# A decode block on one core: the last gate loaded with its siblings, and w2 summed in rows of half a block

## The chip, the cores and the metric

The kernel runs on one core of a Trainium2 chip. The metric is the device time of one execution in microseconds; before the change the median of three runs is 242.71 us (242.71 to 242.87).

## The reference

One decode step of a transformer block for 4 sequences with a model width of 512. A condition vector `c` gives six modulation vectors, the last of which, `gb`, is the gate of the second half:

```python
mod = (_silu(c) @ w_mod).reshape(c.shape[0], 6, 1, -1)
sa, ca, ga, sb, cb, gb = (mod[:, 0], mod[:, 1], mod[:, 2], mod[:, 3], mod[:, 4], mod[:, 5])
h = _layernorm(x, axis=-1) * (1 + ca) + sa
x = x + ga * _A_ref(h, A_k_cache, A_v_cache, A_wq, A_wo)
h = _layernorm(x, axis=-1) * (1 + cb) + sb
x = x + gb * _B_ref(h, B_w1, B_w3, B_w2)
```

`_A_ref` is attention of one new token over the last 2048 positions of a cache, with 32 query heads in 8 groups. `_B_ref` is the feed-forward part, `(silu(h @ w1) * (h @ w3)) @ w2` with a hidden width of 1792. All is fp32.

## The kernel before, in words

The kernel reads 101 MB of weights and cache once and computes little on them. It is written engine by engine: each engine has its own instruction list, and they wait for each other with semaphores. TensorE (PE) multiplies, VectorE (DVE) and ScalarE (ACT) do the rest, SyncE (SP) issues nearly all loads into one queue, which serves them in the order of issue.

**Attention.** The 8 groups go through two large buffers, `KV[0]` and `KV[1]`, in pairs, in a loop on PE (`pair`, L332) and ACT. A buffer is loaded again when the group in it has been used: SP waits for `x_done` (L112, L114, L122, L125). When group 6 is done, SP loads the weights of the second half into `KV[0]` (L123, L124); when group 7 is done, into `KV[1]` (L126 to L129).

**Loads of the second half, in this order.** `wm_in` is three parts of `w_mod` (`ga`, `sb`, `cb`; 3072 KB, semaphore `dm`). `f1_in` is w1 and a piece of w3 (4096 KB, `df1`). `f2_in` is the rest of w3 (3072 KB, `df2`). `gw_in` is the last gate's part of `w_mod` and the first four chunks of w2 (2048 KB, `dw[0]`). The rest of w2 follows in pieces. A chunk of w2 is 128 of its 1792 rows, laid out as 512 columns on 128 partitions (256 KB); `W2_CUTS` counts in half chunks of 256 columns, and the pieces after `gw_in` end at 16, 20, 24, 27 and 28: 1024, 512, 512, 384 and 128 KB.

**The second half on the engines, from L391.** PE multiplies the attention output out (bM), then the three parts of the modulation into bank `bX` (L396 to L400): four steps of k, and in each one matmul for every part, which writes its own group of 32 output rows. ACT copies the three parts (L402), DVE makes `x1`, and DVE and ACT the layer norm (`stats`, `rroot`), which ends in `h`; one step of it is ACT's Square on L156. PE spreads `x1` over 128 rows (below), transposes `h` and, when `h2T` is copied (L424), multiplies by f1 into bank `bQ` (L432) and by f2 into `bA` (L442). Between these, ACT copies `g_sb` (L438) and PE turns it. DVE builds the hidden vector `hidT`; its last step is L467, after PE's transposes of `u_sb`.

**w2 and the end.** A result of 4 rows of 512 uses few of the 128 partitions, so the kernel ends in another form: 8 blocks of 64 columns on 128 rows. `spread` (L263) brings a tensor into that form with 8 short matmuls of 64 columns: for each of the four groups of 32 output rows two, one for each half of a block of 128 columns, with the small constant `same` shifted by `half` as weights. The first 8 chunks of w2 (HEAD) are multiplied in long matmuls of 512 columns into bank `bO` (L486), copied to `y_sb` (L496) and spread into `bX` (L502). The gate `gb_sb` comes from four long matmuls into `bM` (L472), is copied by ACT (L475), spread into `bT` (L498) and copied again (`gbJ`, L500). The remaining chunks go straight into `bX` in rows of half a block: 8 matmuls of 64 columns for each chunk, with `half` of `hidT` as weights (L492); the last chunk is split into two halves, each of 4 such matmuls. PE waits for the semaphore of each piece (`dw`, L479). DVE multiplies by `gbJ`, adds `x1J` (L505, L507), and SP stores the output (L509).

Of the kernel before, what the change touches and what calls it, by code (L numbers as in the profile page):

```python
# [10 lines left out]
B, D, HQ, G, SK, DH, W, FF = 4, 512, 32, 8, 8192, 128, 2048, 1792  # L11
P = 128
# [1 line left out]
NT = 4  # L14
EPS = 1e-5
CHUNKS = [(j, c) for c in range(4) for j in range(4) if c < 2 or j < 3]
HEAD = 8

W2_CUTS = [0, 8, 16, 20, 24, 27, 28]
H = 64  # L20
PAIRS = G // 2
W2_AT = 8192
OUT_SHAPE = (P, H)


# [19 lines left out]
        return (self.sem, self.n)  # L45


def block_kernel(nc, x_in, t0_in, t1_in, kv_in, w_in, wm_in, f1_in, f2_in, gw_in, w2_in, out):
    T, v, s, gp, S = nc.tensor, nc.vector, nc.scalar, nc.gpsimd, nc.sync

    def sems(names):
# [2 lines left out]
    def sb(name, cols, rows=P):  # L54
        return nc.alloc_sbuf_tensor(name, (rows, cols), F32).ap()
# [18 lines left out]
    ident, same, eps = sb("ident", P), sb("same", 48), sb("eps", 1)  # L74
    sc, e1, e2 = sb("sc", 16), sb("e1", 16), sb("e2", 16)
    hT, h2T = sb("hT", 16), sb("h2T", 16)
    Z = sb("Z", B * 28)
    q_sb, p_sb, o_sb, a_sb, y_sb, g_sb, u_sb, gb_sb = [sb(n, 512) for n in "q_sb p_sb o_sb a_sb y_sb g_sb u_sb gb_sb".split()]
    pT = sb("pT", NT * B * 16)
    oT = sb("oT", R * B)  # L80
    MX, MT, NM, NB, SM, ST, LS, LR, LB = [sb(n, 32) for n in "MX MT NM NB SM ST LS LR LB".split()]
    sa_sb, ga_sb, sb_sb, cb_sb = [sb(n, 512, B) for n in "sa_sb ga_sb sb_sb cb_sb".split()]
    xc, sq, xs, h, ag, x1 = [sb(n, 512, B) for n in "xc sq xs h ag x1".split()]
    st1, st2 = sb("st1", 8, B), sb("st2", 8, B)
    eT, dT, rT, sT = [sb(n, 64) for n in "eT dT rT sT".split()]
    hidT = sb("hidT", 16 * 48)
    x1J, gbJ, yt, y = [sb(n, H) for n in "x1J gbJ yt y".split()]
    zero = y_sb

    bS, bQ, bT, bP, bO, bX, bA, bM = [bank(n) for n in "bS bQ bT bP bO bX bA bM".split()]  # L90

# [1 line left out]
    def load(dst, src, sem):  # L93
        S.dma_start(dst, src).then_inc(sem, 16)  # L94
# [25 lines left out]
    load(KV[1][:, 8192:14336], kv_in[G - 1][:, 8192:14336], dva)  # L120
    load(KV[1][:, 14336:], kv_in[G - 1][:, 14336:], dvb)
    S.wait_ge(x_done, G - 1)  # L122
    load(KV[0][:, :6144], wm_in, dm)  # L123
    load(KV[0][:, 6144:14336], f1_in, df1)  # L124
    S.wait_ge(x_done, G)  # L125
    load(KV[1][:, :6144], f2_in, df2)  # L126
    load(KV[1][:, 6144:10240], gw_in, dw[0])
    for a, b, sem in zip(W2_CUTS[1:-1], W2_CUTS[2:], dw[1:]):
        load(KV[1][:, W2_AT + a * 256 : W2_AT + b * 256], w2_in[:, (a - 8) * 256 : (b - 8) * 256], sem)  # L129


    l_eps = L.op(gp.memset(eps, EPS))
# [123 lines left out]
    def mm(o, lhsT, rhs, start=True, stop=True):  # L256
        return T.matmul(o, lhsT, rhs, start=start, stop=stop, skip_group_check=True)  # L257
# [144 lines left out]
    t_ga, t_sb, t_cb = [A.op(s.copy(dst, bX[32 * i : 32 * i + B, :])) for i, dst in enumerate((ga_sb, sb_sb, cb_sb))]  # L402
# [12 lines left out]
    spread(bS, same[:B], x1)  # L415
    A.wait((pe, 5))
    t_x1J = A.op(s.copy(x1J, bS[:, :H]))

    T.wait_ge(V.sem, t_h2[1])
    for k in range(4):  # L420
        ins = T.transpose(bT[:, k * B : (k + 1) * B], h[:, k * P : (k + 1) * P], ident[:B, :B])
    ins.then_inc(pe, 1)
    V.wait((pe, 6))
    t_h2T = V.op(v.tensor_copy(h2T, bT[:, :16]))  # L424

    def view(t_):
# [4 lines left out]
    T.wait_ge(df1, 16)  # L431
    for k in range(4):  # L432
        for j in range(4):
            at = 6144 + k * 2048 + j * 512
            ins = mm(bQ[32 * j : 32 * j + B, :], h2T[:, k * B : (k + 1) * B], KV[0][:, at : at + 512], k == 0, k == 3)
    ins.then_inc(pe, 1)
    A.wait((pe, 7))
    t_g = A.op(s.copy(g_sb, bQ))  # L438
    T.wait_ge(A.sem, t_g[1])
    turn(bP, g_sb, pe)  # L440
# [1 line left out]
    for k in range(4):  # L442
        for j in range(3):
            at = k * 1536 + j * 512
            ins = mm(bA[32 * j : 32 * j + B, :], h2T[:, k * B : (k + 1) * B], KV[1][:, at : at + 512], k == 0, k == 3)
    ins.then_inc(pe, 1)
    A.wait((pe, 8))
    t = A.op(s.activation(view(eT), view(bP)[:, :, :, :B], AF.Exp, scale=-1.0))
    V.wait(t)
    t = V.op(v.tensor_scalar(dT, eT, 1.0, None, op0=ALU.add))  # L450
# [6 lines left out]
    hv = hw[:, :, :, 16 : 16 + B]  # L457
    V.wait(l_z)
    V.op(v.tensor_mul(hv[:, 0:2, 3], view(sT)[:, 0:2, 3], view(bP)[:, 2:4, 3, :B]))
    V.wait((pe, 9))  # L460
    t_u = V.op(v.tensor_copy(u_sb[:96], bA[:96]))
    T.wait_ge(V.sem, t_u[1])
    for c in range(4):
        ins = T.transpose(bS[:, c * P : c * P + 96], u_sb[:96, c * P : (c + 1) * P], ident[:96, :96])
    ins.then_inc(pe, 1)
    V.wait((pe, 10))
    t_hid = V.op(v.tensor_mul(hv[:, :, :3], view(sT)[:, :, :3], view(bS)[:, :, :3, :B]))  # L467


    T.wait_ge(dw[0], 16)  # L470
    for k in range(4):
        ins = mm(bM[32 * k : 32 * k + B, :], sc[:, k * B : (k + 1) * B], KV[1][:, 6144 + 512 * k : 6144 + 512 * (k + 1)])  # L472
    ins.then_inc(pe, 1)
    A.wait((pe, 11))
    t_gb = A.op(s.copy(gb_sb, bM))  # L475
    T.wait_ge(V.sem, t_hid[1])
    for i in range(len(W2_CUTS) - 1):
        if i:
            T.wait_ge(dw[i], 16)  # L479
        for n in range(W2_CUTS[i], W2_CUTS[i + 1]):  # L480
            if n < 26 and n % 2:
                continue
            jj, c = CHUNKS[n // 2]
            if n < 2 * HEAD:
                at, k = W2_AT + n * 256, n // 2
                ins = mm(bO[32 * (k % 4) : 32 * (k % 4) + B, :], hv[:, c, jj, :], KV[1][:, at : at + 512], k < 4, k >= HEAD - 4)  # L486
                continue
            for j in range(4):
                for r in (n % 2,) if n >= 26 else (0, 1):
                    at = W2_AT + (n * 256 + j * H if n >= 26 else n * 256 + j * P + r * H)  # L490
                    w = half(hw[:, c, jj, :], r)
                    ins = mm(bX[32 * j : 32 * j + 32, :H], w, KV[1][:, at : at + H], False, n == 27)  # L492
        if i == 1:
            ins.then_inc(pe, 1)
            V.wait((pe, 12))
            t_y = V.op(v.tensor_copy(y_sb, bO))  # L496
            T.wait_ge(A.sem, t_gb[1])
            spread(bT, same, gb_sb)  # L498
            A.wait((pe, 13))
            t_gb = A.op(s.copy(gbJ, bT[:, :H]))  # L500
            T.wait_ge(V.sem, t_y[1])
            spread(bX, same, y_sb, True, False)  # L502
    ins.then_inc(pe, 1)
    V.wait((pe, 14), t_gb)
    t = V.op(v.tensor_mul(yt, bX[:, :H], gbJ))  # L505
    V.wait(t, t_x1J)
    V.op(v.tensor_add(y, yt, x1J), last)  # L507
# [6 lines left out]
def _layout(i):  # L514
    import numpy as np

    def a(t):
        return np.ascontiguousarray(t)

    k = i["A_k_cache"][:, :, SK - W :, :].reshape(B, G, NT, 512, DH)  # L520
    v = i["A_v_cache"][:, :, SK - W :, :].reshape(B, G, NT, 4, P, DH)
    k = k.transpose(1, 4, 2, 0, 3).reshape(G, P, 8192)
    v = v.transpose(1, 4, 2, 0, 3, 5).reshape(G, P, 8192)
    wm = i["w_mod"].reshape(4, P, 6, 512).transpose(1, 0, 2, 3)
    c = i["c"].reshape(B, 4, P).transpose(2, 1, 0).reshape(P, 16)
# [9 lines left out]
    return {  # L535
        "x_in": a(i["A_x"].reshape(B, D)),
        "t0_in": np.concatenate([c, wm[:, :, 1::-1].reshape(P, 4096)], 1),
        "t1_in": np.concatenate([wq[0], wq[1]], 1),
        "kv_in": np.concatenate([k, v], 2),
        "w_in": np.stack([np.concatenate(p, 1) for p in pairs]),  # L540
        "wm_in": a(wm[:, :, 2:5]).reshape(P, 6144),
        "f1_in": np.concatenate([w1, w3[:, :, 1536:]], 2).reshape(P, 8192),
        "f2_in": a(w3[:, :, :1536]).reshape(P, 6144),
        "gw_in": np.concatenate([a(wm[:, :, 5]).reshape(P, 2048), w2[:, : 4 * D]], 1),
        "w2_in": a(w2[:, 4 * D :]),
    }


# [20 lines left out]
```

## Time and profile before

| | us |
|---|---|
| median of three runs | 242.71 |
| the profiled execution | 242.85 |
| its span, first to last instruction | 241.5 |
| PE busy | 135.7 |
| DVE busy | 38.5 |
| ACT busy | 24.2 |

The profile is of one execution; its times are microseconds from the start of the span. A row of a timeline has the start, the duration, the engine, the line, the operation, the tile written and the tiles read, the shapes and the number of instructions merged into the row; in brackets stands the idle time before it and who ended it. An fp32 matmul shows as two passes, so counts in the profile are twice those in the code (transposes are one pass). A row of an issue list has the number of issues, their size and the median time from issue to landing. A row of a list of stages has the stretch, the busy time of each engine, the granted clock of PE as a share of full speed, the busy share of the DMA engines and GB/s.

### The profile page before, as it was taken

How to read it: one execution, taken by the hardware profiler on the slowest of the kernel's cores; microseconds unless marked ns; L12 is line 12 of the kernel's file. 1: busy time of each engine (PE TensorE's matmuls, PEld its weight loads, DVE VectorE, ACT ScalarE, POOL GpSimd, SP SyncE). 2: the span in 40 equal slices, each digit the busy share in tenths (PEclk: the TensorE clock that was granted, in tenths of full speed). 3: DMA queues.
4: the chain of work that ended last, by engine and by line, in shares of the span. 5: the costliest groups of instructions: out<-in, count | busy, mean ns of one | idle time of the engine just before them, and what ended most of it. 6: DMA issues, size and time to landing. Idle time of an engine off the chain costs nothing. (4 is left out here: it accounts for less than half of the span.)

```text
span 241.5 us, 2424 instructions
## 1 busy us (share of the span) xinstructions
PE 135.7 (56%) x1020; PEld 39.1 (16%) x1020; DVE 38.5 (16%) x126; ACT 24.2 (10%) x51; POOL 2.3 (1%) x15
## 2 busy tenths in 40 slices
PE   3004547818773378176613871757228767674885
PEld 0000121301221012012100120112001222111213
DVE  3003202201200022012000220220002222115121
ACT  2002101100110021001200021011000201122100
POOL 3000000000000000000000000000000000000000
PEclk9999958976589599679965699779957997995899
DMA  7998989899989898999898989998989999999992
GB/s 272 446 501 358 510 361 499 369 423 429 516 358 510 358 510 360 429 434 505 369 499 369 499 369 423 434 510 369 499 347 440 436 406 444 452 431 396 431 400 105
DMA packets 3756, 101.30 MB, mean 419 GB/s; under 512 B 548, under 2 KB 676, under 8 KB 1064
## 3 DMA queue, kind: packets, MB, share of 16 engines
q1 hardware_dynamic: 3600, 99.13, 95.6%
q10 hardware_dynamic: 152, 2.11, 2.1%
q8 instruction: 3, 0.05, 0.1%
q14 instruction: 1, 0.01, 0.0%
HBM read 101.20 MB, written 0.03 MB: 419 GB/s over the span
## 5 line engine op out<-in xcount | busy, mean ns | idle before, releaser
L257 PE MATMUL bS<-KV,Z 128*16 128x512 f32 x256 | 42.7, 827 | 41.1 <-PEq L273 41.1
L257 PE MATMUL bO<-KV,pT 128*16 128x512 f32 x256 | 32.9, 658 | 0.5
L257 PEld LDWEIGHTS bS<-KV,Z 128*16 128x16 f32 x256 | 9.2, 123 | 69.1 <-issue 69.1
L220 DVE TENSOR_REDUCE MX<-bS 128x1 f32<-128x512 f32 x8 | 5.5, 692 | 82.2 <-PE bS L257 82.2
L382 ACT ACTIVATE p_sb<-bS,NB 128x512 f32<-128x512 f32 x8 | 5.5, 687 | 103.7 <-ACTq L373 103.7
L291 PE MATMUL bP<-ident,p_sb 128*128 128x128 f32 x32 | 5.5, 298 | 17.3 <-PEq L273 17.3
L257 PE MATMUL bM<-KV,sc 128*4 128x512 f32 x24 | 5.9, 711 | 16.0 <-DVE sc L190 16.0
L257 PE MATMUL bA<-WP,oT 128*4 128x512 f32 x64 | 10.4, 731 | 4.0 <-PEq L273 4.0
L257 PEld LDWEIGHTS bO<-KV,pT 128*16 128x16 f32 x256 | 8.4, 106 | 23.5 <-issue 23.5
L387 ACT ACTIVATE o_sb<-bO,LB 128x512 f32<-128x512 f32 x8 | 5.5, 687 | 48.9 <-ACTq L373 48.9
L291 PE MATMUL bX<-ident,o_sb 128*128 128x128 f32 x32 | 5.0, 280 | 7.8 <-PEq L273 7.8
L246 DVE TENSOR_REDUCE oT<-bX 128x16 f32<-128x64 f32 x8 | 1.8, 224 | 43.7 <-PE bX L291 43.7
L257 PE MATMUL bQ<-WP,hT 128*4 128x512 f32 x64 | 8.3, 592 | 0.6 <-DVE hT L199 0.6
L291 PEld LDWEIGHTS bP<-ident,p_sb 128*128 128x128 f32 x32 | 3.6, 150 | 24.4 <-issue 24.4
L291 PE MATMUL bT<-ident,q_sb 128*128 128x128 f32 x32 | 5.4, 296 | 3.6 <-PEq L273 3.6
L291 PEld LDWEIGHTS bX<-ident,o_sb 128*128 128x128 f32 x32 | 3.4, 140 | 15.0 <-issue 15.0
L229 DVE COPY pT<-bP 128x256 f32<-128x256 f32 x8 | 3.4, 425 | 14.1 <-PE bP L291 14.1
L257 PE MATMUL bQ<-KV,h2T 128*4 128x512 f32 x32 | 5.4, 842 | 0.3 <-DVE h2T L424 0.3
L291 PEld LDWEIGHTS bT<-ident,q_sb 128*128 128x128 f32 x32 | 3.6, 147 | 7.5 <-issue 7.2
L257 PE MATMUL bX<-KV,sc 128*4 128x512 f32 x24 | 4.4, 592 | 0.0
L257 PEld LDWEIGHTS bM<-KV,sc 128*4 128x4 f32 x24 | 0.9, 96 | 20.9 <-DVE sc L190 17.6
L204 DVE TENSOR_REDUCE Z<-bT 128x16 f32<-128x64 f32 x8 | 1.8, 225 | 14.5 <-PE bT L291 14.2
(104 smaller groups left out, 69.2 us busy)
## 6 DMA issues: line engine op xcount, KB each, us to landing
WP<-w_in SPq DMA_DIRECT2D x3, 4096.0 KB, 19.7
KV<-kv_in SPq DMA_DIRECT2D x1, 4096.0 KB, 24.0
KV<-f_in SPq DMA_DIRECT2D x1, 4096.0 KB, 25.6
KV<-kv_in SPq DMA_DIRECT2D x1, 3072.0 KB, 30.8
KV<-wm_in SPq DMA_DIRECT2D x1, 3072.0 KB, 16.3
KV<-f_in SPq DMA_DIRECT2D x1, 3072.0 KB, 18.8
KV<-t_in SPq DMA_DIRECT2D x1, 2056.0 KB, 12.3
WP<-t_in ACTq DMA_DIRECT2D x1, 2048.0 KB, 12.5
```

Of the source, the lines that this page charges most:

```text
L204: v.tensor_reduce(Z.rearrange("p (b i) -> p b i", b=B)[:, :, 12 : 12 + R], bT.rearrange("p (r k i) -> p i r k", r=R, k=4)[:, :B], axis=AX. ...
L220: t = V.op(v.reduce_max(MX[:, 0:1], bS, axis=AX.X))
L229: v.tensor_copy(pT.rearrange("p (t b c r) -> p c b t r", t=NT, b=B, c=4), bP.rearrange("p (c b i) -> p c b i", c=4, b=B)[:, :, :, :16].rea ...
L246: V.op(v.tensor_reduce(oT.rearrange("p (r b) -> p r b", r=R), diag, axis=AX.X, op=ALU.add), ot_ok)
L257: return T.matmul(o, lhsT, rhs, start=start, stop=stop, skip_group_check=True)
L291: ins = T.transpose(dst[:, c * P : (c + 1) * P], src[:, c * P : (c + 1) * P], ident)
L382: A.op(s.activation(p_sb, bS, AF.Exp, bias=NB[:, 0:1], accum_out=SM[:, 0:1]), p_ok)
L387: A.op(s.mul(o_sb, bO, LB[:, 0:1]), o_ok)
```

## The change

The last gate's part of `w_mod` is loaded with the other three in `wm_in`, which has 4096 KB now and fills `KV[0]` together with f1. Its four matmuls go into `bX` beside those of the other parts, as the fourth group of output rows; ACT copies it after the other three, PE spreads it right after `x1`, and ACT copies it into `gbJ` after `x1J`. The tail loses its four matmuls and its spread. w2 begins right behind f2 in `KV[1]`, and its pieces are 16, 8, 3 and 1 half chunks: 2048, 1024, 384 and 128 KB, one load fewer in all. The long matmuls into `bO`, the copy `y_sb` and its spread are gone: all 14 chunks go into `bX` in rows of half a block, 112 matmuls of 64 columns where there were 48. The tile that clears bank `bA` at the start (`zero`) is one of its own.

```diff
-HEAD = 8
-
-W2_CUTS = [0, 8, 16, 20, 24, 27, 28]
+W2_CUTS = [0, 16, 24, 27, 28]
-W2_AT = 8192
+W2_AT = 6144
...
-    load(KV[0][:, :6144], wm_in, dm)
-    load(KV[0][:, 6144:14336], f1_in, df1)
+    load(KV[0][:, :8192], wm_in, dm)
+    load(KV[0][:, 8192:], f1_in, df1)
     S.wait_ge(x_done, G)
     load(KV[1][:, :6144], f2_in, df2)
-    load(KV[1][:, 6144:10240], gw_in, dw[0])
-    for a, b, sem in zip(W2_CUTS[1:-1], W2_CUTS[2:], dw[1:]):
-        load(KV[1][:, W2_AT + a * 256 : W2_AT + b * 256], w2_in[:, (a - 8) * 256 : (b - 8) * 256], sem)
+    for a, b, sem in zip(W2_CUTS[:-1], W2_CUTS[1:], dw):
+        load(KV[1][:, W2_AT + a * 256 : W2_AT + b * 256], w2_in[:, a * 256 : b * 256], sem)
...
     T.wait_ge(dm, 16)
     for k in range(4):
-        for i in range(3):
-            at = (3 * k + i) * 512
+        for i in range(4):
+            at = (4 * k + i) * 512
             ins = mm(bX[32 * i : 32 * i + B, :], sc[:, k * B : (k + 1) * B], KV[0][:, at : at + 512], k == 0, k == 3)
...
-    t_ga, t_sb, t_cb = [A.op(s.copy(dst, bX[32 * i : 32 * i + B, :])) for i, dst in enumerate((ga_sb, sb_sb, cb_sb))]
+    t_ga, t_sb, t_cb, t_gb = [A.op(s.copy(dst, bX[32 * i : 32 * i + B, :])) for i, dst in enumerate((ga_sb, sb_sb, cb_sb, gb_sb))]
...
     t_x1J = A.op(s.copy(x1J, bS[:, :H]))
+    T.wait_ge(A.sem, t_gb[1])
+    spread(bO, same[:B], gb_sb)
+    A.wait((pe, 6))
+    t_gbJ = A.op(s.copy(gbJ, bO[:, :H]))
...
-    T.wait_ge(dw[0], 16)
-    for k in range(4):
-        ins = mm(bM[32 * k : 32 * k + B, :], sc[:, k * B : (k + 1) * B], KV[1][:, 6144 + 512 * k : 6144 + 512 * (k + 1)])
-    ins.then_inc(pe, 1)
-    A.wait((pe, 11))
-    t_gb = A.op(s.copy(gb_sb, bM))
     T.wait_ge(V.sem, t_hid[1])
     for i in range(len(W2_CUTS) - 1):
-        if i:
-            T.wait_ge(dw[i], 16)
+        T.wait_ge(dw[i], 16)
         for n in range(W2_CUTS[i], W2_CUTS[i + 1]):
             if n < 26 and n % 2:
                 continue
             jj, c = CHUNKS[n // 2]
-            if n < 2 * HEAD:
-                at, k = W2_AT + n * 256, n // 2
-                ins = mm(bO[32 * (k % 4) : 32 * (k % 4) + B, :], hv[:, c, jj, :], KV[1][:, at : at + 512], k < 4, k >= HEAD - 4)
-                continue
             for j in range(4):
                 for r in (n % 2,) if n >= 26 else (0, 1):
                     at = W2_AT + (n * 256 + j * H if n >= 26 else n * 256 + j * P + r * H)
                     w = half(hw[:, c, jj, :], r)
-                    ins = mm(bX[32 * j : 32 * j + 32, :H], w, KV[1][:, at : at + H], False, n == 27)
-        if i == 1:
-            ins.then_inc(pe, 1)
-            V.wait((pe, 12))
-            t_y = V.op(v.tensor_copy(y_sb, bO))
-            T.wait_ge(A.sem, t_gb[1])
-            spread(bT, same, gb_sb)
-            A.wait((pe, 13))
-            t_gb = A.op(s.copy(gbJ, bT[:, :H]))
-            T.wait_ge(V.sem, t_y[1])
-            spread(bX, same, y_sb, True, False)
-    ins.then_inc(pe, 1)
-    V.wait((pe, 14), t_gb)
+                    ins = mm(bX[32 * j : 32 * j + 32, :H], w, KV[1][:, at : at + H], n == 0 and r == 0, n == 27)
+    ins.then_inc(pe, 1)
+    V.wait((pe, 12), t_gbJ)
```

How the changed program stands on the queues, word for word, is shown where it is used in the prediction; for SP the stretch of loads changes like this. Before, from the three parts of `w_mod` on:

```order
12 L94 DMA KV<-wm_in 128x6144
13 L94 DMA KV<-f_in 128x8192
14 L94 DMA KV<-f_in 128x6144
15 L94 DMA KV<-gw_in 128x4096
16 L94 DMA KV<-w_in 128x2048
17 L94 DMA KV<-w_in 128x1024 x2
18 L94 DMA KV<-w_in 128x768
19 L94 DMA KV<-w_in 128x256
```

And after, on SP in the same place (w_in is w2, f_in are f1 and f2):

```order
12 L92 DMA KV<-wm_in 128x8192
13 L92 DMA KV<-f_in 128x8192
14 L92 DMA KV<-f_in 128x6144
15 L92 DMA KV<-w_in 128x4096
16 L92 DMA KV<-w_in 128x2048
17 L92 DMA KV<-w_in 128x768
18 L92 DMA KV<-w_in 128x256
```

The gate's 2048 columns have moved from the fourth load into the first, and the two loads of 1024 columns have become part of one of 2048.

More of the change, by code (lines that the diff above doesn't have):

```diff
@@ L45, in op, with block_kernel @@
         return (self.sem, self.n)
-def block_kernel(nc, x_in, t0_in, t1_in, kv_in, w_in, wm_in, f1_in, f2_in, gw_in, w2_in, out):
+def block_kernel(nc, x_in, t0_in, t1_in, kv_in, w_in, wm_in, f1_in, f2_in, w2_in, out):
     T, v, s, gp, S = nc.tensor, nc.vector, nc.scalar, nc.gpsimd, nc.sync
@@ L77, in block_kernel @@
     Z = sb("Z", B * 28)
-    q_sb, p_sb, o_sb, a_sb, y_sb, g_sb, u_sb, gb_sb = [sb(n, 512) for n in "q_sb p_sb o_sb a_sb y_sb g_sb u_sb gb_sb".split()]
+    q_sb, p_sb, o_sb, a_sb, zero, g_sb, u_sb = [sb(n, 512) for n in "q_sb p_sb o_sb a_sb zero g_sb u_sb".split()]
     pT = sb("pT", NT * B * 16)
@@ L81, in block_kernel @@
     MX, MT, NM, NB, SM, ST, LS, LR, LB = [sb(n, 32) for n in "MX MT NM NB SM ST LS LR LB".split()]
-    sa_sb, ga_sb, sb_sb, cb_sb = [sb(n, 512, B) for n in "sa_sb ga_sb sb_sb cb_sb".split()]
+    sa_sb, ga_sb, sb_sb, cb_sb, gb_sb = [sb(n, 512, B) for n in "sa_sb ga_sb sb_sb cb_sb gb_sb".split()]
     xc, sq, xs, h, ag, x1 = [sb(n, 512, B) for n in "xc sq xs h ag x1".split()]
@@ L87, in block_kernel @@
     x1J, gbJ, yt, y = [sb(n, H) for n in "x1J gbJ yt y".split()]
-    zero = y_sb
     bS, bQ, bT, bP, bO, bX, bA, bM = [bank(n) for n in "bS bQ bT bP bO bX bA bM".split()]
@@ L422, in block_kernel @@
     ins.then_inc(pe, 1)
-    V.wait((pe, 6))
+    V.wait((pe, 7))
     t_h2T = V.op(v.tensor_copy(h2T, bT[:, :16]))
@@ L433, in block_kernel @@
         for j in range(4):
-            at = 6144 + k * 2048 + j * 512
+            at = 8192 + k * 2048 + j * 512
             ins = mm(bQ[32 * j : 32 * j + B, :], h2T[:, k * B : (k + 1) * B], KV[0][:, at : at + 512], k == 0, k == 3)
     ins.then_inc(pe, 1)
-    A.wait((pe, 7))
+    A.wait((pe, 8))
     t_g = A.op(s.copy(g_sb, bQ))
@@ L446, in block_kernel @@
     ins.then_inc(pe, 1)
-    A.wait((pe, 8))
+    A.wait((pe, 9))
     t = A.op(s.activation(view(eT), view(bP)[:, :, :, :B], AF.Exp, scale=-1.0))
@@ L459, in block_kernel @@
     V.op(v.tensor_mul(hv[:, 0:2, 3], view(sT)[:, 0:2, 3], view(bP)[:, 2:4, 3, :B]))
-    V.wait((pe, 9))
+    V.wait((pe, 10))
     t_u = V.op(v.tensor_copy(u_sb[:96], bA[:96]))
@@ L465, in block_kernel @@
     ins.then_inc(pe, 1)
-    V.wait((pe, 10))
+    V.wait((pe, 11))
     t_hid = V.op(v.tensor_mul(hv[:, :, :3], view(sT)[:, :, :3], view(bS)[:, :, :3, :B]))
-    T.wait_ge(dw[0], 16)
-    for k in range(4):
-        ins = mm(bM[32 * k : 32 * k + B, :], sc[:, k * B : (k + 1) * B], KV[1][:, 6144 + 512 * k : 6144 + 512 * (k + 1)])
-    ins.then_inc(pe, 1)
-    A.wait((pe, 11))
-    t_gb = A.op(s.copy(gb_sb, bM))
     T.wait_ge(V.sem, t_hid[1])
     for i in range(len(W2_CUTS) - 1):
-        if i:
-            T.wait_ge(dw[i], 16)
+        T.wait_ge(dw[i], 16)
         for n in range(W2_CUTS[i], W2_CUTS[i + 1]):
@@ L540, in _layout @@
         "w_in": np.stack([np.concatenate(p, 1) for p in pairs]),
-        "wm_in": a(wm[:, :, 2:5]).reshape(P, 6144),
+        "wm_in": a(wm[:, :, 2:6]).reshape(P, 8192),
         "f1_in": np.concatenate([w1, w3[:, :, 1536:]], 2).reshape(P, 8192),
         "f2_in": a(w3[:, :, :1536]).reshape(P, 6144),
-        "gw_in": np.concatenate([a(wm[:, :, 5]).reshape(P, 2048), w2[:, : 4 * D]], 1),
-        "w2_in": a(w2[:, 4 * D :]),
+        "w2_in": a(w2),
     }
```

## The prediction

> **What bounds the kernel now.** I read the page first: where the DMA stands through the span, and the chain that ended last.
>
> ```profile
> span 241.5 us, 2424 instructions
> DMA  7998989899989898999898989998989999999992
> q8 instruction: 3, 0.05, 0.1%
> DMA KV<-w_in 11%; SPq L94 1%; PE bX L257 0%; PE bX L291 0%; DVE yt L505 0%; DVE y L507 0%
> ```
>
> The transfers are busy from the first slice to the last but one, and the chain ends in a transfer of w2. So I asked for the chain in order of time; its last pieces are:
>
> ```profile
> 211.26 27.45 DMA KV<-w_in
> ...
> 238.75 0.73 PE bX L257 x32
> 239.49 0.02 issue
> 239.51 0.24 DVE yt L505
> ...
> 239.77 0.23 DVE y L507
> ```
>
> The sixth load after the last attention group (w2, half chunks 24 to 26) is issued at 211.26 and lands at 238.71. PE then has 16 matmuls left, which the profile shows as 32 passes, two for each fp32 matmul, and the output follows. So the end is a landing plus a fixed 2.8 us. PE alone can move the end only if it comes to those 16 matmuls later than their data. Next the traffic of the last microseconds, by stage:
>
> ```profile
> 235.00:236.00 1.00, 0.79 (x12) 0.22 (x9) 0.00 (x0) 0.00 (x0) 0.00 (x0) 1.00 1.01 397
> 236.00:237.00 1.00, 0.57 (x20) 0.28 (x15) 0.63 (x1) 0.21 (x1) 0.00 (x0) 1.00 0.86 309
> 237.00:238.00 1.00, 0.88 (x60) 0.88 (x64) 0.07 (x1) 0.00 (x0) 0.00 (x0) 1.00 0.16 62
> 238.00:239.00 1.00, 0.76 (x51) 0.60 (x44) 0.00 (x0) 0.00 (x0) 0.00 (x0) 1.00 0.05 17
> ```
>
> The last column is GB/s. The flow falls from 397 to 62 and 17 while the last pieces still wait to land: for its last two microseconds the queue is nearly empty, and a few late transfers set the landing (rival 3).
>
> Then the issues on SP, from two stretches of the timeline, and the time from issue to landing:
>
> ```profile
> 194.51 0.33 SPq L94 DMA_DIRECT2D KV<-wm_in  x1
> 194.88 0.43 SPq L94 DMA_DIRECT2D KV<-f_in  x1
> ```
>
> ```profile
> 208.99 0.33 SPq L94 DMA_DIRECT2D KV<-f_in  x1
> 209.36 0.43 SPq L94 DMA_DIRECT2D KV<-gw_in  x1
> 209.84 2.33 SPq L94 DMA_DIRECT2D KV<-w_in  x5
> ```
>
> ```profile
> KV<-f_in SPq DMA_DIRECT2D x1, 4096.0 KB, 25.6
> KV<-wm_in SPq DMA_DIRECT2D x1, 3072.0 KB, 16.3
> KV<-f_in SPq DMA_DIRECT2D x1, 3072.0 KB, 18.8
> KV<-gw_in SPq DMA_DIRECT2D x1, 2048.0 KB, 23.4
> KV<-w_in SPq DMA_DIRECT2D x1, 1024.0 KB, 25.4
> KV<-w_in SPq DMA_DIRECT2D x1, 128.0 KB, 27.3
> ```
>
> Issue plus time gives the landings: wm 210.8, f1 220.5, f2 227.8, gw 232.8, the 1024 KB of w2 235.2; 238.7 comes from the chain; and the 128 KB, the fifth of five issues 0.475 apart (211.74), 239.0. All were issued long before the queue reached them, so nothing in this stretch waits for SP, and one landing follows the other at a rate: 4096 KB in 9.7 us, which is 2.42 for 1024 KB; the piece of 1024 KB itself 2.4 to 2.5.
>
> **The change, part by part.** First the loads. The bytes are the same. The last gate's 1024 KB move ahead of f1 and f2, so dm, df1 and df2 land 2.42 later: 213.2, 222.9 and 230.2. The first piece of w2 has as many bytes ahead of it, itself counted, as the old 1024 KB piece: 235.2. The next 1024 KB come in one load where there were two of 512: 235.2 + 2.5 = 237.7. What this saves at the end: 512 + 512 + 384 KB took 238.71 - 235.2 = 3.5 us. At that mean rate two pieces of 512 KB cost 2.5, and with the 384 KB taken as three times the last 128 KB (0.3 each) 2.6. The same bytes now pass at 2.42. So the last landings come 0.1 us earlier (bounds 0.0 and 0.2): 238.6 and 238.9. SP issues one load fewer, which is worth nothing, as it is 27 us ahead.
>
> Now whether PE still arrives in time. Its rows, from three stretches, the first two of them for durations alone:
>
> ```profile
> 189.25 3.63 PE L257 MATMUL bO<-KV,pT 128*16 128x512 f32 x32
> ```
>
> ```profile
> 211.67 4.01 PE L257 MATMUL bX<-KV,sc 128*4 128x512 f32 x22
> ...
> 221.51 5.45 PE L257 MATMUL bQ<-KV,h2T 128*4 128x512 f32 x32 [0.27 <-DVE h2T L424]
> 227.67 0.66 PE L291 MATMUL bP<-ident,g_sb 128*128 128x128 f32 x4 [0.72 <-ACT g_sb L438]
> 228.26 3.61 PE L257 MATMUL bA<-KV,h2T 128*4 128x512 f32 x24
> ...
> 236.12 0.44 PE L257 MATMUL bT<-gb_sb,same 128*32 128x64 f32 x16
> ...
> 237.37 1.15 PE L257 MATMUL bX<-KV,hidT 128*32 128x64 f32 x64
> 238.75 0.72 PE L257 MATMUL bX<-KV,hidT 128*32 128x64 f32 x32 [0.24 <-DMA KV<-w_in]
> ```
>
> The fourth part of w_mod: 12 matmuls become 16, but the new four write the fourth group of 32 output rows. Three groups (bA, 24 passes) took 3.61 and four groups (bO, 32 passes) 3.63, so it rides along for 0.02; the other bound, 8 passes one after another at 4.01/22, is 1.5. I take 3.63. Before, bX ended at 215.68; now it starts on dm at 213.25 and ends at 216.88, 1.2 us later.
>
> ScalarE and VectorE between bX and h2T:
>
> ```profile
> 215.75 0.57 ACT L402 COPY ga_sb<-bX 4x512 f32<-4x512 f32 x1 [7.56 <-PE bX L257]
> ...
> 216.95 0.58 ACT L402 COPY cb_sb<-bX 4x512 f32<-4x512 f32 x1
> 218.03 0.72 ACT L156 ACTIVATE sq<-x,st 4x512 f32<-4x512 f32 x1 [0.51 <-DVE st L154]
> ```
>
> ```profile
> 221.28 0.17 DVE L424 COPY h2T<-bT 128x16 f32<-128x16 f32 x1 [0.68 <-PE bT L421]
> 233.26 0.20 DVE L467 TENSOR_TENSOR hidT<-sT,bS 128x48 f32<-128x48 f32 x1 [0.64 <-PE bS L464]
> ```
>
> The copy of the gate (0.6) is queued on ScalarE ahead of the Square on L156, which had 0.51 us of idle time before it: 0.1 of the copy lies on the path. So h2T comes 1.3 later, and bQ could start at 221.51 + 1.3 = 222.8; f1 lands at 222.9 and decides. The spread of the gate (0.44) and its second copy (0.2) stand ahead of the transposes of h on PE, and ahead of g_sb on ScalarE; PE idles 2.3 us and ScalarE over 7 us there, which hides both; without that cover they would cost 0.6.
>
> bQ from 222.9, with the 5.45 it had at half clock, ends at 228.4. From its end (226.96) to bA was 1.30 us: PE is at bA at 229.7, and f2 lands only at 230.2, so PE waits 0.5 us there. From bA's start to the end of hid on L467 was 233.46 - 228.26 = 5.20: hid is ready at 235.4, 2.0 later than before. The first piece of w2 has landed by then.
>
> Now w2. Before and after, PE's order from the modulation on (bX<-KV,sc is w_mod, gb_sb the last gate, hidT the hidden vector, KV the loaded weights):
>
> ```order
> 23 L257 MATMUL bX<-KV,sc 4x512 x12
> 24 L257 MATMUL bS<-x,same 32x64 x8
> ...
> 30 L257 MATMUL bM<-KV,sc 4x512 x4
> 31 L257 MATMUL bO<-KV,hidT 4x512 x8
> 32 L257 MATMUL bT<-gb_sb,same 32x64 x8
> 33 L257 MATMUL bX<-y_sb,same 32x64 x8
> 34 L257 MATMUL bX<-KV,hidT 32x64 x48
> ```
>
> ```order
> 23 L254 MATMUL bX<-KV,sc 4x512 x16
> 24 L254 MATMUL bS<-x,same 32x64 x8
> 25 L254 MATMUL bO<-gb_sb,same 32x64 x8
> ...
> 30 L254 MATMUL bS<-ident,u_sb 128x96 x4
> 31 L254 MATMUL bX<-KV,hidT 32x64 x112
> ```
>
> Out of the tail go bM, bO, both spreads and the copy of y_sb in between; 64 short matmuls come in, so that 224 short passes stand behind hid. Their pace: 64 took 1.15 and 32 took 0.72, so 32 more cost 0.43, 13.4 ns each; with 0.22 taken off the 1.15 for the last one's own length it is 14.5 ns. I take 14.5. From 235.45 the first 128 passes end at 237.3, ahead of the second piece (237.7). Then 64 passes, 0.93, to 238.65: level with the landing of the third at 238.6. The last 32 follow as before. **The end is still that landing, 0.1 us earlier**, with PE some 0.35 us short of deciding: 192 passes from hid take 2.8 us, so hid may come up to 235.8.
>
> Sum against the profiled execution: span 241.5 - 0.1 = 241.4. With the 1.35 us outside the span (242.85 less 241.5) that is 242.75; this execution lies 0.14 above the median, so 242.6 for the median. A change under 0.2% (0.49 us) can't be told from none here.
>
> **Rivals.** 1. *The rows of w2 make PE the bound.* A short group runs slower for each pass: the spread bT took 0.44 for 16, 27.5 ns. PE decides once a pass costs over (238.6 - 235.45)/192 = 16.5 ns. At 18 ns (1.15/64, nothing taken off) the end is 235.45 + 224 x 0.018 + 0.2 = 239.7, against 239.47 for bX's end before: +0.2. At 27.5 it is 241.8: +2.3, 245.0. Against it stands the row of 64. The Trainium skill, TensorE: Matmul & The Clock Gate, section Back-to-back issue gap, speaks against this change: it gives a floor of about 25 ns for matmuls of up to 64 columns; by that the 224 passes take 5.6 us (estimate from that page). The trace does not agree: 64 passes of 64 columns in 1.15 us. Chance 0.09, of which 0.06 over the 0.49 us.
>
> 2. *The clock.* PE waits longer for dm, and bX could start at half clock.
>
> ```profile
> 211.20:215.70 4.50, 4.46 (x26) 0.87 (x26) 0.00 (x0) 0.00 (x0) 0.00 (x0) 1.00 0.97 411
> 218.50:225.20 6.70, 4.27 (x24) 1.20 (x28) 2.02 (x7) 1.06 (x5) 0.00 (x0) 0.50 0.97 416
> ```
>
> The granted clock is 1.00 in bX's stretch and 0.50 in bQ's, and bQ took 5.45 against bO's 3.63. If bX lost the same 1.8: bQ at 224.6, bA at 231.4, hid at 236.6, the 192 passes done at 239.4 where before the last 32 could start at 238.7: +0.7, 243.4. Against it: PE idles only about 1.1 us ahead of bX. Chance 0.05.
>
> 3. *The late end of the flow goes away.* At 62 and 17 GB/s some 80 KB take two microseconds. If larger pieces let everything land 1.5 us earlier, df2 no longer decides: bA starts at 229.7, hid is ready at 234.9, and 224 passes end at 234.95 + 3.25 + 0.2 = 238.4: 1.1 less, 241.6. Against it: the bytes and the four last stages are nearly the same. Chance 0.07.
>
> 4. *PE's longer program is loaded late.* The instruction queue moved 3 packets, 0.1% of 16 engines' span: 0.1% x 16 x 241.5 / 3 = 1.3 us each. PE gets 48 more matmuls. One more packet on the engine that lands last would cost up to 1.1 beside the gain: 243.8. The Trainium skill, Runtime: NRT & Kernel Launch, section Instruction fetch mechanics, says that code comes in blocks of 256 instructions fetched while the last runs, mostly hidden; no row here shows a stall. Chance 0.05.
>
> **How the numbers follow.** Forecast 0.74; rivals 0.09, 0.05, 0.07, 0.05. Faster is rival 3: 0.07. Slower is 0.06 + 0.04 + 0.04 = 0.14. Same: 0.79. The range: from 242.2, which leaves out most of rival 3, to 243.3, which takes in bX in sequence (+1.5, by the arithmetic of rival 2 +0.4) and the mild cases of rivals 1 and 2.
>
> **What would show it.** Right: bX<-KV,sc starts near 213.3 behind a DMA and takes 3.6; bQ starts at 222.9; PE waits about half a microsecond for f2; the 112 matmuls show two waits for DMA, and the chain ends in KV<-w_in near 238.6. Wrong: the chain runs through PE from hid to the end without a DMA (rival 1 or 2, told apart by the pace of the passes and the granted clock), or PE idles in w2 for code (rival 4).

## The result, and the profile after

The changed kernel takes 244.2 us (median of six runs, 243.68 to 244.95) against 242.8 for the kernel before on the same chips: a ratio of 1.0057, with a 95% interval of 1.0038 to 1.0077. It is slower, by 1.4 us. The forecast was 242.6, with a range up to 243.3.

The profiled execution took 244.95 us with a span of 243.6, so 2.1 more than the span of before (241.5). First the page: the instruction queue, and the chain by engine.

```profile
q8 instruction: 4, 0.07, 0.1%
...
PE 9%; DMA 8%; ACT 2%; DVE 1%; issue 1%
```

The chain no longer ends in a transfer of w2, and "issue" (an engine that waited for nothing that the profile shows) is 1% of it. The same chain in order of time, its second half (start, duration, what):

```profile
193.27 19.88 DMA KV<-wm_in
213.15 0.04 issue
213.19 5.16 PE bX L254 x32
...
224.14 6.51 PE bQ L254 x32
...
237.15 2.04 PE bX L254 x124
239.19 0.78 issue
239.97 1.64 PE bX L254 x94
241.60 0.02 issue
241.62 0.24 DVE yt L484
```

The last transfer in it is `w_mod`, which lands at 213.15. Everything behind is PE with what ScalarE and VectorE do between its groups, and there is a hole of 0.78 us inside w2. The transfers had landed as forecast. SP's issues and the times to landing:

```profile
193.64 13.28 SPq L92 DMA_DIRECT2D KV<-f_in  x2
206.96 1.85 SPq L92 DMA_DIRECT2D KV<-w_in  x4
```

```profile
KV<-f_in SPq DMA_DIRECT2D x1, 4096.0 KB, 29.1
...
KV<-f_in SPq DMA_DIRECT2D x1, 3072.0 KB, 23.4
...
KV<-w_in SPq DMA_DIRECT2D x1, 2048.0 KB, 28.0
...
KV<-w_in SPq DMA_DIRECT2D x1, 1024.0 KB, 30.0
KV<-w_in SPq DMA_DIRECT2D x1, 384.0 KB, 30.4
KV<-w_in SPq DMA_DIRECT2D x1, 128.0 KB, 30.3
```

The first f load goes out at 193.64 and lands at 222.7, the second, issued at 206.5 (0.43 before the end of its row), at 229.9. The four of w2, a quarter of 1.85 us apart, land at 235.0, 237.4, 238.3 and 238.7. The forecast had 222.9, 230.2, 235.2, 237.7, 238.6 and 238.9. PE in the same stretch, with the idle time ahead of each group in brackets:

```profile
208.82 1.02 PE L254 MATMUL bM<-a_sb,same 128*4 128x512 f32 x2 [0.81 <-DVE a_sb L391]
213.19 5.11 PE L254 MATMUL bX<-KV,sc 128*4 128x512 f32 x32 [3.35 <-DMA KV<-wm_in]
...
224.14 6.45 PE L254 MATMUL bQ<-KV,h2T 128*4 128x512 f32 x32 [0.27 <-DVE h2T L425]
...
237.15 2.04 PE L254 MATMUL bX<-KV,hidT 128*32 128x64 f32 x127 [0.30 <-DVE hidT L468]
239.97 1.62 PE L254 MATMUL bX<-KV,hidT 128*32 128x64 f32 x97 [0.78 <-issue]
```

And by stages (the last three columns are the granted clock, the DMA share and GB/s):

```profile
209.00:213.20 4.20, 0.85 (x3) 0.01 (x2) 0.00 (x0) 0.00 (x0) 0.00 (x0) 0.96 0.99 417
213.20:218.40 5.20, 5.10 (x32) 0.84 (x32) 0.00 (x0) 0.02 (x1) 0.00 (x0) 0.71 1.05 454
...
224.10:230.70 6.60, 6.45 (x32) 1.02 (x32) 0.00 (x0) 0.03 (x1) 0.00 (x0) 0.56 0.99 425
...
239.20:240.00 0.80, 0.04 (x4) 0.04 (x5) 0.00 (x0) 0.00 (x0) 0.00 (x0) 1.00 0.00 0
```

Two things are wrong with PE. **The clock:** it idles 3.35 us ahead of bX, the granted clock falls to a mean of 0.71, and bX takes 5.11 where 3.63 was forecast; bQ at 0.56 takes 6.45. hid is ready at 237.1 instead of 235.4. **The stop:** after 127 passes of w2 PE does nothing for 0.78 us. The next pass still belongs to the first piece of w2, which landed at 235.0, and no bytes move meanwhile. A pass is two instructions here (a weight load and a matmul), so the stop comes 254 instructions into w2. The trace has a 16 KB packet of the instruction queue at 237.26, right after w2's start, which ends at 238.59, 1.38 us before PE goes on. That points to code that comes too late; whether it is so, the experiments had to show.

### The profile page after: what moved, and what is told of

Its sections match the earlier page's. It is cut to its first block, busy times and chain, and to the rows that moved or that the text cites. A ratio compares the mean times of both kernels' runs of the same rounds, so it can differ in the third digit from the quotient of the medians.

```text
span 243.6 us, 2613 instructions
## 1 busy us (share of the span) xinstructions
PE 135.2 (56%) x1116; PEld 39.9 (16%) x1116; DVE 37.8 (16%) x125; ACT 24.0 (10%) x51; POOL 2.3 (1%) x15
## 5 line engine op out<-in xcount | busy, mean ns | idle before, releaser
L254 PE MATMUL bO<-KV,pT 128*16 128x512 f32 x256 | 30.0, 610 | 0.5
L288 PE MATMUL bP<-ident,p_sb 128*128 128x128 f32 x32 | 6.2, 328 | 17.2 <-PEq L270 17.2
L254 PE MATMUL bA<-WP,oT 128*4 128x512 f32 x64 | 10.9, 759 | 1.7 <-PEq L270 1.6
L254 PEld LDWEIGHTS bO<-KV,pT 128*16 128x16 f32 x256 | 7.7, 102 | 21.8 <-issue 21.8
L254 PE MATMUL bX<-KV,sc 128*4 128x512 f32 x32 | 5.1, 795 | 3.3 <-DMA KV<-wm_in 3.3
L254 PE MATMUL bQ<-KV,h2T 128*4 128x512 f32 x32 | 6.5, 980 | 0.3 <-DVE h2T L425 0.3
L254 PE MATMUL bX<-KV,hidT 128*32 128x64 f32 x224 | 3.7, 221 | 1.1 <-issue 0.8
```

What stands on the lines that cost most here:

```text
L288: ins = T.transpose(dst[:, c * P : (c + 1) * P], src[:, c * P : (c + 1) * P], ident)
```

## The experiments

The two theories: **late code** (the 224 short passes run through a block of code faster than the next arrives) and **the clock** (the longer wait for `w_mod` costs bX and bQ their clock). The rival to both was that rows of half a block, or the new order of the loads, are slow in themselves. e4 and e3 each take one half of the change alone; most of the others add throwaway matmuls to one of these kernels: they write bank `bA` with zeros, before anything that is read is put there. A tiny one (16 columns) is four instructions; a full one has 512 columns and takes 1.0 us. The kernel before had medians of 242.77 to 242.83 on the same chips throughout.

**e4_rows: the rows alone.** All of w2 in rows of half a block, in the kernel before; its loads and its gate stay.

```diff
-            if n < 2 * HEAD:
-                at, k = W2_AT + n * 256, n // 2
-                ins = mm(bO[32 * (k % 4) : 32 * (k % 4) + B, :], hv[:, c, jj, :], KV[1][:, at : at + 512], k < 4, k >= HEAD - 4)
-                continue
...
-            t_y = V.op(v.tensor_copy(y_sb, bO))
-            spread(bX, same, y_sb, True, False)
```

> The part on the rows alone: loads, pieces and the gate's place as before, but all 14 chunks of w2 in rows of half a block, without bO, its copy and its spread. Theory: hid is ready at 233.5 as before, the rows have 2 us of slack behind the landings, so neither their pace nor a stop of 0.8 us reaches the end: 242.7 to 242.9. Reading in which the rows themselves are too slow: 243.5 or more.

Measured: 245.19 (244.04 to 245.53), ratio 1.0085 (1.0063 to 1.0106). The expectation missed by over 2 us, and this half alone is slower than the whole change. Its PE in w2:

```profile
235.12 1.12 PE L257 MATMUL bX<-KV,hidT 128*32 128x64 f32 x62 [0.18 <-DMA KV<-w_in]
...
238.79 0.26 PE L257 MATMUL bT<-gb_sb,same 128*32 128x64 f32 x1 [2.30 <-issue]
238.80 2.82 PE L257 MATMUL bX<-KV,hidT 128*32 128x64 f32 x96
```

```profile
236.50:238.80 2.30, 0.01 (x2) 0.00 (x1) 0.00 (x0) 0.00 (x0) 0.00 (x0) 0.97 0.22 79
238.80:241.70 2.90, 2.82 (x97) 2.58 (x96) 0.04 (x1) 0.21 (x1) 0.00 (x0) 0.50 0.02 6
```

A stop of 2.30 us in the middle of a spread of the gate, whose data had been there for long, and half clock behind it: the last 96 passes take 2.82 us, about 27 ns each with 0.2 taken off for the last one's length, where 224 take 3.41 at full clock (e1 below). A packet of code at 236.32 ends 1.40 us before PE goes on, as in the changed kernel.

**e7_rows_pad: the same with 15 tiny matmuls ahead of the transposes of h.** They add work and lie where PE idles. What they change is where in the code the blocks end: 60 instructions earlier.

```diff
+    for _ in range(15):
+        mm(bA[:32, :16], zero[:, :32], zero[:, :16])
```

> The rows alone with 15 tiny matmuls more (60 instructions, in PE's idle time ahead of the transposes of h), so that instruction 713 is passed while PE works on f2 and not in the middle of w2, and its packet can come in time. Code theory: the stop of 2.3 us after 143 passes is gone or under 0.5, the clock stays at 1.00 in w2, and the time falls from 245.2 to 242.8 to 243.5, although PE has more to do. Rival (rows of half a block are slow in themselves): 245.2 or more.

Measured: 242.88 (242.55 to 243.14), ratio 1.0001 (0.9993 to 1.001), as the code theory had it: 2.3 us less than without them, by adding useless work.

```profile
236.58 0.69 PE L257 MATMUL bX<-KV,hidT 128*32 128x64 f32 x32
237.81 0.69 PE L257 MATMUL bX<-KV,hidT 128*32 128x64 f32 x32 [0.54 <-DMA KV<-w_in]
238.78 0.68 PE L257 MATMUL bX<-KV,hidT 128*32 128x64 f32 x32 [0.27 <-DMA KV<-w_in]
```

No stop; each piece is waited for again, and the end is the landing, as in the kernel before. So the stop is one of code, and **rows cost nothing in themselves**. The page counts four instruction packets with and without the padding: what counts is when they come. With the padding, the packet for which PE stood still in e4 (236.32) lies at 231.18, before w2's first pass at 233.69.

**e1_pad: the change, with 8 tiny matmuls (32 instructions) ahead of the wait for dm.**

```diff
+    for _ in range(8):
+        mm(bA[:32, :16], zero[:, :32], zero[:, :16])
     T.wait_ge(dm, 16)
```

> The changed kernel with 8 tiny matmuls (16 columns, thrown away) ahead of the wait for dm, where PE idles: they add 32 instructions to PE's program and move the place of the stop after 127 passes in w2. Theory (two causes: PE's program isn't there in time in w2, 0.8 us, and PE at half clock behind the wait for dm, the rest): the gap of 0.78 us in w2 is gone, bX and bQ still run partly at half clock, and the time falls by 0.8 us, to about 243.4. Rival A (the clock alone, and the gap is something of the data or of the chip's timing): the gap stays, 244.2. Rival B (the program alone, the clock costs nothing): 242.7, level with the kernel before.

Measured: 243.21 (242.47 to 246.05), ratio 1.0031 (1.0004 to 1.0059); the profiled execution took 243.72.

```profile
213.03 5.07 PE L254 MATMUL bX<-KV,sc 128*4 128x512 f32 x32 [2.60 <-DMA KV<-wm_in]
...
223.94 6.43 PE L254 MATMUL bQ<-KV,h2T 128*4 128x512 f32 x32 [0.27 <-DVE h2T L427]
...
236.94 3.41 PE L254 MATMUL bX<-KV,hidT 128*32 128x64 f32 x224 [0.30 <-DVE hidT L470]
```

The stop is gone here and the slow clock is not, so this execution prices the two in that order: its span is 242.4, 1.0 over the forecast 241.4 (the clock), and 1.2 under the changed kernel's 243.6 (the stop, 0.2 of it because hid came that much earlier). Its twelve times fall into six up to 242.75 and six from 243.67; only one of the upper six has a profile. The median lies in the gap between the groups, where no time does, so that it comes near the expected 243.4 is luck.

**e3_gate: the loads and the gate alone**, with w2 in long matmuls and short rows as before (HEAD = 8, six pieces). **e5_gate_short** is the same with one wait moved to an earlier instruction, so that PE's program is one instruction shorter; it tested whether a fourth packet beside the output made e3 slow, since e3's output took 2.7 us (issued at 241.06, span 243.8) where others take 1.5. The first edit is against the changed kernel, the second against e3.

```diff
+HEAD = 8
-W2_CUTS = [0, 16, 24, 27, 28]
+W2_CUTS = [0, 8, 16, 20, 24, 27, 28]
...
+            if n < 2 * HEAD:
+                at, k = W2_AT + n * 256, n // 2
+                ins = mm(bM[32 * (k % 4) : 32 * (k % 4) + B, :], hv[:, c, jj, :], KV[1][:, at : at + 512], k < 4, k >= HEAD - 4)
+                continue
...
+            t_y = V.op(v.tensor_copy(y_sb, bM))
...
+            spread(bX, same, y_sb, True, False)
```

```diff
+        if c == 1:
+            T.wait_ge(dw[0], 16)
...
-        T.wait_ge(dw[i], 16)
+        if i:
+            T.wait_ge(dw[i], 16)
```

> The part on the gate alone: w_mod's last part comes with the others as in the change, but w2 is multiplied as before (8 chunks in long matmuls, copied and spread; six pieces). PE's program is as long as before. Theory: dm still lands 2.4 us later and PE still waits for it and turns cold, so hid is ready some 3 us later than before; behind it stand 4.4 us of work as before, so PE ends about where the changed kernel does: 243.5 to 244.2. Rival B (the program alone costs the time): 242.6 to 242.8. A third reading (the rows alone cost the time): 242.7.

> The gate alone once more, with one PE instruction fewer (a wait for w2's first piece is put on an earlier instruction): 969 instructions on PE as in the kernel before, where the first run of the gate alone had 970 and a fourth 16 KB instruction packet, which came at 241.6 beside the output's transfer and held the output back by 1.2 us. Code theory (packets of PE's code come when PE passes every 256th instruction, here 713 and 969 of the built program): three packets again, the output lands 1.5 us after its issue, and the median falls from 243.8 to 243.0 to 243.4, the rest being the clock behind the wait for dm. Rival (the number of instructions has nothing to do with it): 243.8 as before.

Measured: e3 243.8 (243.36 to 246.29), ratio 1.0059 (1.0033 to 1.0084); e5 244.24 (243.65 to 244.89), ratio 1.0054 (1.0042 to 1.0066). e5's expectation, 243.0 to 243.4, is a miss: it moved three packets instead of four in its profile, its output took 1.5 us, and it was no faster, so the packet beside the output is not what the median of this half hangs on. Its PE:

```profile
212.70 5.13 PE L256 MATMUL bX<-KV,sc 128*4 128x512 f32 x32 [3.08 <-DMA KV<-wm_in]
...
223.68 6.46 PE L256 MATMUL bQ<-KV,h2T 128*4 128x512 f32 x32 [0.27 <-DVE h2T L427]
```

e3's median is in the expected range, but its profile is not as expected: bX kept its clock and only bQ lost it. hid came at 235.9, and PE still ended a microsecond later than in the kernel before (239.47), since the old tail behind hid is longer than the new; the slow output adds another 1.2 in this execution:

```profile
212.76 3.62 PE L256 MATMUL bX<-KV,sc 128*4 128x512 f32 x32 [0.72 <-DMA KV<-wm_in]
...
222.91 6.50 PE L256 MATMUL bQ<-KV,h2T 128*4 128x512 f32 x32 [0.96 <-DMA KV<-f_in]
...
235.96 1.90 PE L256 MATMUL bM<-KV,hidT 128*4 128x512 f32 x16 [0.30 <-DVE hidT L470]
...
238.92 1.59 PE L256 MATMUL bX<-KV,hidT 128*32 128x64 f32 x96
```

From hid to PE's end it takes 4.55 us there (235.96 to 240.51), 3.41 in rows (e1). So the gate's half needs the rows, and each half alone is slower than before, for a reason of its own. How much of e3's and e5's medians is the clock and how much the longer tail, no run separates.

**e6_one_more: the kernel before with one tiny matmul more**, to see whether four instructions push the old program over a block's end at its output.

```diff
+    mm(bA[:32, :16], zero[:, :32], zero[:, :16])
     T.wait_ge(V.sem, t_h2[1])
```

> The kernel before with one tiny matmul more (16 columns, thrown away, 4 instructions, in PE's idle time ahead of the transposes of h): 973 instructions on PE. Code theory: a fourth instruction packet near the end, which runs beside the output's transfer: up to 1.2 us slower, 243.2 to 244.0, in some executions less. Rival: a matmul of 16 columns in idle time costs nothing, 242.8.

Measured: 242.85 (242.57 to 243.32), ratio 1.0003 (0.9994 to 1.0011), with three packets as before. A miss: no fourth packet came in its profile, so the blocks do not end where they were reckoned to, and what a packet beside the output costs this kernel was not tested.

**e2_warm: the change with PE kept busy** by seven full matmuls (two each ahead of dm, behind bX and ahead of the transposes of h, one ahead of f2) and one tiny one: 32 instructions, as many as e1. **e8_warm_pad: the same with eight tiny ones**, 60 instructions. The edit of e8, the first piece ahead of dm and the others at the other three places; e2 has one tiny matmul there instead of eight:

```diff
+    def fill(n):
+        for _ in range(n):
+            mm(bA, zero[:, :P], zero)
+
+    fill(2)
+    for _ in range(8):
+        mm(bA[:32, :16], zero[:, :32], zero[:, :16])
...
+    fill(2)
...
+    fill(2)
...
+    fill(1)
```

> The changed kernel with as many added instructions as the run with tiny matmuls, but 7 of the matmuls are full ones (128x128 by 512 columns, thrown away) in PE's waits: two ahead of dm, two after bX, two ahead of the transposes of h, one ahead of f2. PE stays busy enough to keep its full clock. Theory: bX takes 3.6 and bQ 3.6 us at clock 1.00, hid is ready near 235.5 where it was 237.1, the gap in w2 is gone, PE waits for the last pieces of w2 again, and the time is 242.4 to 242.7. Rival A (clock alone): the gap stays, 243.2. Rival B (program alone, the clock costs nothing): the same as with tiny matmuls.

> The changed kernel with the 7 full matmuls that keep the clock and 28 more instructions of tiny ones, so that instruction 713 is passed another 28 instructions earlier, at the start of bA. The run with less had two groups of times, 242.3 to 242.6 and 244.3 to 244.8. If the slow group is a packet that comes late for instruction 969, it is gone here and all times are 242.3 to 242.8, under the kernel before. If the slow group has another cause (the packet that follows, beside the output, or the landings), it stays.

Measured: e2 243.46 (242.31 to 244.82), ratio 1.0032 (1.001 to 1.0054), in two groups of six, 242.31 to 242.63 and 244.29 to 244.82, the profiled one 242.31 (the expectation, 242.4 to 242.7, holds for the lower group alone); e8 **242.51 (242.40 to 242.72)**, ratio 0.9989 (0.998 to 0.9997), with no second group. e8's PE:

```profile
214.50 3.59 PE L254 MATMUL bX<-KV,sc 128*4 128x512 f32 x29
...
223.78 3.62 PE L254 MATMUL bQ<-KV,h2T 128*4 128x512 f32 x32 [0.27 <-DVE h2T L434]
...
230.23 3.61 PE L254 MATMUL bA<-KV,h2T 128*4 128x512 f32 x24 [0.61 <-DMA KV<-f_in]
...
235.49 3.76 PE L254 MATMUL bX<-KV,hidT 128*32 128x64 f32 x224 [0.30 <-DVE hidT L478]
```

With the clock held, f2 is waited for 0.61 and hid is ready at 235.4, as forecast, and the time is the forecast's 242.6 less 0.1. The fillers hold bX back by 1.3 us, which the wait for f2 takes up. With 32 instructions the clock's cure alone left half of the executions near 244.4; with 60 none. That the upper group of e2 had the stop fits its size, but none of them has a profile.

**e9_pad60: the change with the 60 instructions as 15 tiny matmuls ahead of dm, e10_warm_first: two full and 13 tiny ones there, e11_pad_late: the 15 tiny ones ahead of the transposes of h**, which leaves the wait for dm as the change made it. They ask what the clock costs once the code is in time. e9 and e11 hold the first edit (at their two places), e10 the second:

```diff
+    for _ in range(15):
+        mm(bA[:32, :16], zero[:, :32], zero[:, :16])
```

```diff
+    for _ in range(2):
+        mm(bA, zero[:, :P], zero)
+    for _ in range(13):
+        mm(bA[:32, :16], zero[:, :32], zero[:, :16])
```

> The changed kernel with 60 instructions of tiny matmuls ahead of the wait for dm and no full ones: PE's code is in time as in the run with 7 full matmuls and the same 1222 instructions (242.51), but the clock is left to itself. Theory of two causes: no stop in w2 in any execution, no group of times at 244.3 or more, and what is left over 242.5 is the clock: bX and bQ partly at half clock, hid ready at 236 to 237, 243.0 to 243.8. Rival (the clock costs nothing, all of the loss was code): 242.5.

> As the run with 60 instructions of tiny matmuls, but two of them are replaced by full matmuls ahead of the wait for dm, and nothing is added in the later waits. Theory: bX keeps the full clock and takes 3.6, bQ still starts at half clock after two idle times of 2 us and takes 5.4 to 6.5; hid is ready 1.0 to 1.5 earlier than with tiny ones, near 235.5 to 236, within or just over what the landings of w2 hide: 242.5 to 243.0. Rival (bX's clock doesn't matter): the same time as with tiny ones alone.

> The same 60 instructions as in e9, but behind the modulation, ahead of the transposes of h, so that the wait for dm is left as the change made it and only the place of the code boundaries moves. Both: no stop inside w2. Theory of two causes: bX behind the long wait is at half clock again (5.1 us, as in e1) in executions where attention ends early, hid comes 0.5 to 1 us later than 235.4, and the median lies between e9's 242.59 and 243.7; with bX at 5.1 and bQ at 5.5 to 6.4 an execution takes 243.2 to 243.7. Theory that late code is all: 242.5 to 242.8 in every execution, with bX at 3.6 or with hid still in time.

Measured: e9 242.59 (242.44 to 243.95; two of twelve over 243.8), ratio 1.0001 (0.9988 to 1.0014); e10 242.61 (242.43 to 244.06; one of eleven over 244), ratio 1.0 (0.9989 to 1.0012); e11 242.67 (242.34 to 244.24; four of twelve over 243.5), ratio 1.0011 (0.9995 to 1.0026). The code in time takes 1.5 to 1.6 us off the changed kernel's median. For e9 the theory of two causes had 243.0 to 243.8: a miss. Its median and e11's lie where the rival had them (242.5; 242.5 to 242.8), though not every execution does. So code in time wins back all that the median had lost, and what is left for the clock is a tail of executions 1 to 1.6 us longer: four in e11, two in e9, one in e10, too few to rank by how much the wait for dm is filled, and none in e8. e10 came out as e9 and doesn't tell what bX's clock is worth: its fillers hold bX back to 214.49. The profiled e11, 242.51, is not of the tail, and has no stop:

```profile
202.51 4.89 PE L254 MATMUL bO<-KV,pT 128*16 128x512 f32 x32
...
211.27 1.02 PE L254 MATMUL bM<-a_sb,same 128*4 128x512 f32 x2 [0.81 <-DVE a_sb L391]
213.08 3.62 PE L254 MATMUL bX<-KV,sc 128*4 128x512 f32 x32 [0.78 <-DMA KV<-wm_in]
...
222.88 4.91 PE L254 MATMUL bQ<-KV,h2T 128*4 128x512 f32 x32 [0.80 <-DMA KV<-f_in]
...
235.36 3.78 PE L254 MATMUL bX<-KV,hidT 128*32 128x64 f32 x224 [0.29 <-DVE hidT L470]
```

Here attention ends at 211.3, as in the kernel before, and bX waits only 0.78 us and keeps its clock. In the changed kernel's profile it ended 2.4 us earlier, and the reason is in its last group (bO, 4.89 here):

```profile
201.33 3.62 PE L254 MATMUL bO<-KV,pT 128*16 128x512 f32 x32
```

So an execution of these profiles either loses the clock in the last attention group, where nothing waits for it, or reaches the wait for dm early, idles there for 2.6 to 3.4 us (after, e1, e5) and loses it in bX. In the profiles with 0.5 to 0.8 us of idle (e3, e9, e11), bX took 3.62. That the long executions of e9, e10 and e11 are of the second kind fits all of this, and is not shown, since no profile fell on one.

The traces' record of the granted clock says more about which kind an execution is. In each of the 13 profiles the clock changes only at points a multiple of 3.41 us apart, and where these points fall in the program differs from one profile to the next. From 170 us on, a full clock was halved at every such point (37 times) at which PE had been busy for 1.27 us or less of the 3.41 before it, and kept at every one at which it had been busy for 1.40 or more, but for one (e11 at 222.12, with 2.2 busy, half of it tiny matmuls). The three profiles that lost bX's clock have a point in the wait for dm, at 212.84, 212.60 and 212.40, with 0.41, 1.24 and 0.63 us busy before it (after, e1, e5); in e9, e3 and e11 the last points ahead of bX were 210.28, 211.69 and 211.88, with 1.67, 2.20 and 2.20. So, as far as these profiles go, which executions pay depends on where these points fall; no run moved them.

## Why the prediction was wrong

**Right: the loads.** Every landing came where the sum put it, 0.05 to 0.3 us early, and the fourth group of bX rides along: 3.62 for four groups at full clock (e9, e11).

**Right: rival 1 is refuted.** 224 passes take 3.41 us (e1), 14.3 ns each after taking off 0.2 for the last one's length, against the 14.5 taken. The floor of about 25 ns in the Trainium skill, TensorE: Matmul & The Clock Gate, section Back-to-back issue gap, is not what these passes show, which write four groups of 32 output rows in turn; only at half clock do they come to 27 (e4). Nor did rival 3 happen: e8 sits at 242.5, not at 241.6.

**Wrong: "PE some 0.35 us short of deciding".** The step rests on hid at 235.4, and that on bX at 3.63 behind an idle time of "about 1.1 us". The 1.1 was taken from one execution, in which attention happened to end at 211.2 with its last group at half clock (halved at 201.36). dm was moved 2.4 us later, and where attention ends 2.4 earlier PE idles 3.35. This is rival 2's mechanism with a larger price than it was given: bX lost the 1.5 and bQ another 1.0 beyond the 5.45 assumed; hid came at 237.1 where the rival said 236.6. By e1 it costs 1.0 us of span when it happens, and if the long executions of e9 and e11 (two and four of twelve) are of this kind, it happens in fewer than half of them.

**Wrong: rival 4's place, price and chance.** This is the step on which the median hangs: PE's code stands at nothing in the sum, and as a rival it was one more packet on the engine that lands last, at 0.05. The extra packet (four instead of three) was there, at 241.01, and the output behind it took 1.5 us as before. PE stopped for the packet ahead of that one, at 237.26; the kernel before has one at 236.76 too, and its profile shows no stop. The price is 0.78 us idle, 1.0 in the end with the restart (4.44 from w2's start to its end against 3.41), and 2.30 idle in e4. The sum's own numbers did not show it: a packet was 1.3 us by its estimate (1.0 to 1.1 in the trace of the kernel before, 1.33 and 1.07 where PE stopped), and 128 passes at 14.5 ns, a block of 256 instructions, last 1.86, so the packet looks to be in time. What was missing is the time behind the packet: PE goes on only 1.4 us after its end, 2.7 after its start (2.5 in e4), and that is more than 1.86. The Trainium skill, Runtime: NRT & Kernel Launch, section Instruction fetch mechanics, calls the crossing of a block "mostly hidden"; e4 against e7 shows 2.3 us that were not. The prediction's own signs of being wrong, a chain through PE from hid on and PE idle in w2 for code, both came.

**What the forecast's time was worth.** 242.6 is what the change takes when both are cured (e8: 242.51, the fastest kernel here, faster than before by 0.11%, interval 0.03 to 0.2%, less than the 0.2% under which the prediction told no change from none). The path at the end is a little other than forecast: in e8, e9 and e11 the chain leaves the DMA at the landing of the 1024 KB of w2 (237.5 to 237.6), and PE runs the last 96 passes without waiting for the third piece, level with it, as the sum had said. So the change as such brings next to nothing, as was argued, and loses 1.4 us on PE: the stop in the median, the clock in some of the executions.

What stays open: what places the 3.41 us points against the program, what sets the moment at which a packet starts (in e4 2.5 us after w2's first pass, in the changed kernel 0.1), how the changed kernel's other five executions divide between stop and clock, since one of six has a profile, and whether the upper groups of e1 and e2 had the stop.

## What to carry to other kernels

A long run of short matmuls can outrun its own code: set the time of 256 instructions (1.86 us here) against the time from a packet's start to the engine's going on (2.5 to 2.7 here), not against the packet alone, and see that the blocks change where the engine waits anyway. A load moved up delays the first engine that waits for another; price that engine's clock at the earliest moment it can arrive, not at the one of a single profile. If a row says that PE has 0.35 us to spare, the half-clock price of every group ahead of it (1.5 to 2.8 us here) belongs in the range.

## What the runs showed of the hardware that was not expected

Adding 15 useless matmuls took 2.3 us off a kernel (e4, 245.19; e7, 242.88), and 60 instructions of them 1.6 us off the changed one (244.2; e9, 242.59). A 16 KB packet of code took 0.9 to 1.3 us in these traces, and PE went on 1.4 us after its end, both times that it stopped (after, e4). PE went to half clock in idle times of 2.6, 3.1 and 3.35 us ahead of bX and in the stop of 2.30 in e4, and kept the full clock through 0.5 to 0.8 ahead of bX and through the stop of 0.78; but the length of the idle time does not decide alone, since the clock changed only at points 3.41 us apart, by PE's busy time before them (halved at 1.27 us or less, from 170 us on). Behind a lost clock a group of 32 passes of 512 columns took 4.9 to 6.5 us instead of 3.6.
